# Score rounds one and two of the segment-attention groups two slots earlier in the hand-written order

## The chip, the cores and the metric

The kernel runs on one core of one Trainium2 chip. The metric is the device time of one execution in microseconds. A profile of one execution on the same chip shows every instruction of the engines: TensorE (PE, with its weight loads as PEld), VectorE (DVE), ScalarE (ACT), GpSimd (POOL) and SyncE (SP), which issues the transfers.

## The reference

Four layers run one after the other on x of 2048 tokens by 640 (A, B, A, B), each with a layer norm before it and a residual around it. The change touches only A, attention in four segments of 512 tokens with 32 heads of 20 columns:

```python
for s in range(N):                                  # N = 4 segments of L = 512
    logits = jnp.einsum('bhqd,bhkd->bhqk', qs, ks) * scale + mask
    p = _softmax(logits, axis=-1)
    a_dot = jnp.einsum('bhqk,bhkd->bhqd', p, vs)
    pq = phi(qs)
    num = jnp.einsum('bhld,bhde->bhle', pq, M)
    den = jnp.einsum('bhld,bhd->bhl', pq, z)[..., None] + 1e-06
    outs.append(g * (num / den) + (1.0 - g) * a_dot)
    pk = phi(ks)
    M = M + jnp.einsum('bhld,bhle->bhde', pk, vs)
    z = z + jnp.einsum('bhld->bhd', pk)
return o @ wo
```

The mask is causal within a segment, phi is t + 1 above zero and exp(t) below, g is a gate per head. B (a recurrent attention in 64 steps) is left as it is.

## The kernel before

Layer A takes each segment in 8 groups of four heads, 32 groups in all (`NGR`), and each group in two units, pairs of heads: unit p belongs to group p // 2. The time of a group is cut into four slots. The loop runs over 34 values of g, two halves and two phases, so its slot number is 4g + 2·half + ph; the last two values of g have no group of their own and only finish what is open.

In every slot the loop does its score rounds and then the `filler`, the other work listed for that slot.

Score rounds. For each unit the scores are computed twice. The first time (kind S, rounds 0 to 2, `s_mm` and `s_max`) queries lie on the partitions, and VectorE takes the row maxima. The maxima go through GpSimd (`negmax_rows`) into two spare columns, and `q_with_max` turns Q back with them, giving the tile q2, of which the maximum is a part (the second turn of Q: one matmul with the identity, then four that add the maxima, then a copy). The second time (kind T, rounds 0 to 2, `t_round` and `t_exp`) keys lie on the partitions, TensorE multiplies K's turn with q2, ScalarE takes the exponential into the unit's probability tile PT, and the part on the diagonal is masked. `VISITS` lists which rounds come in which phase: S2, S0, T0 in phase 0, S1, T1, T2 in phase 1. All six use the same three score buffers in PSUM (`psx`). PT comes from the pool `up`, which has three buffers.

Value products. `pv(g)` multiplies both PT tiles of a group with V: 40 matmuls, head by head, so the first 20 read the tile of the first unit only. `norm(g)` then divides and gates on VectorE and GpSimd.

Filler. `SLOTS` says what each slot holds besides: the projections of the next group (QP, KV0, KV1) and the turn of its K (KT), the second turn of Q (Q2), the state's update (UP) and its use (NUM), the value products (PV) of two groups ago, and for the groups 12 to 15, 20 to 23 and 28 to 31 the write-out of a finished 128-token tile of the segment before (otps, YP0, YP1). All of these share two small PSUM buffers (`pg`). `seg_step` puts the loading, norm and turn of the next segment into the first half of a segment's groups.

Order. TensorE runs in the order in which the program is written. ScalarE, VectorE and GpSimd each run in an order by key: the slot number in which the work is written, plus an offset by kind (`A_LAGS`). For ScalarE that gives within slot 3: exponential one, the copy of K's turn, exponential two, the copy of the value products; in slot 0 exponential zero and the copy of Q; in slot 1 exponential one, the copy of q2, exponential two. Waits for data and for buffers are put in by the framework; a tile that finds no free buffer waits for the last reader of the one whose place it takes.

Of the kernel before, what the change touches and what calls it, by code (L numbers as in the profile page):

```python
# [265 lines left out]
def layer_A(nc, tc, C, W, x_src, x_dst, src_is_bf16, nseg=4, out_bf16=False, xb_dst=None, load_w=None, side_loads=None):  # L266
# [4 lines left out]
    NGR = 8 * nseg  # L271
    KOFF = (0, 640, 1024, 512)
    assert not out_bf16
    with ExitStack() as ctx:
# [177 lines left out]
        def k_turn(g):  # L452
            KT_ = pg.tile([128, 4, 128], BF16, name="a_KT", tag="pg")
            for tt in range(4):
                nc.tensor.transpose(KT_[:, tt, :], Kn[g % 2][:, tt, :, :].rearrange("p j s -> p (j s)"), C.identb[:])
            kT = qp4.tile([128, 512], BF16, name="a_kT")
            K("kT").scalar.copy(kT[:], KT_[:].rearrange("p t k -> p (t k)"))
            GS[g]["kT"] = kT
# [15 lines left out]
        def no_tile(step):  # L474
            if step not in NOs:
                NOs[step] = wk.tile([128, 2, 4, 4, 21], F32, name="a_no", tag="a_no")
            return NOs[step]
# [62 lines left out]
        def q_with_max(g):  # L540
            s_ = GS[g]
            N_ = NM[g % 2]
            Q2 = pg.tile([128, 512], F32, name="a_Q2", tag="pg")
            nc.tensor.matmul(Q2[:], lhsT=C.identb[:], rhs=s_["qT"][:], start=True, stop=False, skip_group_check=True)
            for qc in range(4):
                nc.tensor.matmul(Q2[:, 128 * qc:128 * qc + 128], lhsT=N_[:, qc, :, :].rearrange("p j s -> p (j s)"), rhs=C.identb[:],
                                 start=False, stop=(qc == 3), skip_group_check=True)
            q2 = wk.tile([128, 512], BF16, name="a_q2")
            Z = K("q2")
            (Z.vector.tensor_copy if g == NGR - 1 else Z.scalar.copy)(q2[:], Q2[:])  # L550
            s_["q2"] = q2
# [4 lines left out]
        def t_round(p, r, Y):  # L556
            g, pr = divmod(p, 2)
            s_ = GS[g]
            if r == 0:
                s_[("PT", pr)] = up.tile([128, 2, 1280], BF16, name="a_PT", tag="PT")  # L560
            q2, kT, PT = s_["q2"], s_["kT"], s_[("PT", pr)]
            parts = (((0, 0, 512),), ((3, 0, 128), (1, 128, 384)), ((2, 0, 256),))[r]
            width, diag = ((512, 1), (512, 2), (256, 1))[r]
            for n_, (kc, o, w_) in enumerate(parts):
                for e in range(2):
                    j = 2 * pr + e
                    rows = slice(32 * j, 32 * j + 32)
                    nc.tensor.matmul(Y[:, e, o:o + w_], lhsT=kT[rows, 128 * kc:128 * kc + 128], rhs=q2[rows, 128 * kc:512],
                                     start=True, stop=True, tile_position=(32 * j, 0), skip_group_check=True)

        def t_exp(p, r, Y):
            g, pr = divmod(p, 2)
            PT = GS[g][("PT", pr)]
            width, diag = ((512, 1), (512, 2), (256, 1))[r]
            b = 512 * r
            K(f"exp{r}").scalar.activation(out=PT[:, :, b:b + width], in_=Y[:, :, 0:width], func=ACT.Exp, scale=SC)
            dv = PT[:, :, b:b + 128 * diag].rearrange("p e (a q) -> p e a q", q=128)
            if p == 2 * NGR - 1 and r:
                K("dsel").vector.tensor_tensor(out=dv, in0=dv, in1=C.keep[:].unsqueeze(1).unsqueeze(1).to_broadcast([128, 2, diag, 128]), op=ALU.min)
                return  # L580
            K("sel").gpsimd.affine_select(out=dv, in_=dv, pattern=[[0, 2], [0, diag], [1, 128]], compare_op=ALU.is_ge,
                                    fill=0.0, base=0, channel_multiplier=-1)

        def pv(g):
            s_ = GS[g]
            va = s_["va"]
            PV = pg.tile([128, 4, 4, 32], F32, name="a_PV", tag="pg")
            for j in range(4):
                PT = s_[("PT", j // 2)]
                for qc in range(4):  # L590
                    for kc in range(qc + 1):
                        o = KOFF[kc] + 128 * (qc - (kc if kc != 1 else 1))
                        nc.tensor.matmul(PV[:, qc, j, :], lhsT=PT[:, j % 2, o:o + 128], rhs=va[:, kc, j, :],
                                         start=(kc == 0), stop=(kc == qc), skip_group_check=True)
            if g >= NGR - 2:
                s_["osb"] = PV
                return
            K("osb").scalar.copy(no_tile(g + 2)[:, 1], PV[:, :, :, 0:21])
# [78 lines left out]
        K.base = None  # L677

        TPS = (((0, 0), (1, 0), (1, 2)), ((0, 3), (2, 1), (2, 2)), ((1, 3), (3, 0), (3, 3)), ((2, 3), (4, 1), (4, 2)))
        SLOTS = (('otps', 'QP', 'UP'), ('Q2', 'KV0', 'NUM'), ('KV1', 'YP0'), ('KT', 'PV', 'YP1'))  # L680
        VISITS = (('S2', 'S0', 'T0'), ('S1', 'T1', 'T2'))
        OUT_LAG = 4

# [8 lines left out]
        def item(what, g):  # L692
            no, Go = divmod(g - OUT_LAG, 8)
            out = no >= 1 and Go < 4
            if what == "UP" and 0 <= g - 1 < NGR:
                state_up(g - 1)
            elif what == "QP" and g + 1 < NGR:
                proj_q(g + 1)
            elif what == "Q2" and 0 <= g - 1 < NGR - 1:
                q_with_max(g - 1)  # L700
            elif what in ("KV0", "KV1") and g + 1 < NGR:
                proj_kv(g + 1, int(what[2]))
            elif what == "NUM" and g < NGR:
                phi_k(g)
                state_num(g)
            elif what == "KT" and g + 1 < NGR:
                k_turn(g + 1)
            elif what == "PV" and 0 <= g - 2 < NGR:
                pv(g - 2)
                norm(g - 2)  # L710
            elif what == "otps" and out:
                out_stage_a(no - 1, Go)
            elif what in ("YP0", "YP1") and out:
                out_stage_b(no - 1, Go, (int(what[2]),))

        def filler(g, slot):
            K.base = 4 * g + slot + 0.3
            for what in SLOTS[slot]:
                item(what, g)
            if g == NGR and slot == 0:  # L720
                q_with_max(g - 1)
            seg_step(g // 8, g % 8, slot)

        def last_turns(c0, c1):
# [26 lines left out]
        for g in range(NGR + 2):  # L751
            n, G = divmod(g, 8)
            for half in range(2):
                p, tp = 2 * g + half, 2 * g + half - 3
                for ph in range(2):
                    K.base = 4 * g + 2 * half + ph
                    todo = []
                    for what in VISITS[ph]:
                        kind, r = what[0], int(what[1])
                        if kind == "X":  # L760
                            X = s_mask(p, r) if g < NGR else t_tile()
                            if g < NGR:
                                todo.append(("S", p, r, X, 0))
                            if 0 <= tp - 1 < 2 * NGR:
                                todo.append(("T", tp - 1, r, X, 256))
                        elif kind == "S" and g < NGR:
                            todo.append((kind, p, r, s_mask(p, r), 0))
                        elif kind == "T" and 0 <= tp < 2 * NGR:
                            todo.append((kind, tp, r, t_tile(), 0))
                    for step in range(2):  # L770
                        for kind, p_, r, X, o0 in todo:
                            if step == 0 and g >= NGR and (kind, p_) != ("T", 2 * NGR - 3):
                                unread(2)
                            f = (s_mm, s_max)[step] if kind == "S" else (t_round, t_exp)[step]
                            f(p_, r, X, *((o0,) if o0 else ()))
                    if g < NGR and half == 1 and ph == 1:
                        negmax_rows(g)
                    if g == NGR + 1 and half == 1 and ph == 0:
                        last_turns(0, 4)
                        for tt in range(4):  # L780
                            last_oT(tt, 0, 4, K("last").vector if tt < 2 else nc.scalar)
                    filler(g, 2 * half + ph)
                    if side_loads is not None and g < NGR:
                        side_loads[0](4 * g + 2 * half + ph, GS[g]["kT"])
# [651 lines left out]
```

## Time and profile before

| | us |
|---|---|
| median of 3 runs | 2411.46 |
| lowest, highest | 2410.05, 2413.7 |
| the profiled execution | 2409.91 |
| its span in the trace | 2408.0 |

Busy over the whole span: TensorE 2289.4 us (95%), VectorE 1881.2 (78%), ScalarE 1417.7 (59%), GpSimd 750.4 (31%). The two A layers and the two B layers differ: in the page's rows of 40 equal slices ScalarE is at nine tenths in the A layers and at four tenths in B. In timeline rows the columns are start and length in us, engine, line, operation, written tile and what it is read from, shapes, and in brackets idle time of the engine before it and what ended that. `a_T` is a T score tile, `a_S` an S score tile, `a_PT` a probability tile (written by the exponential), `a_Q` and `a_q` the second turn of Q and its copy, `a_KT` and `a_kT` the turn of K and its copy, `a_PV` the value products, `a_no` the copy of those (or of the state's product `a_NUM`), `a_QP` the projection of Q, `a_YP` and `a_otps` the write-out. An exponential 128x1024 wide belongs to round zero or one, 128x512 to round two.

### The profile page before, as it was taken

Reading aid. Unit: us, or ns where it says so; the run is one execution under the profiler, and the core shown is the slowest. Engines: PE = TensorE matmul, PEld = TensorE weight load, DVE = VectorE, ACT = ScalarE, POOL = GpSimd, SP = SyncE. Lnnn points to the kernel's source line nnn. Section 1 sums busy time; section 2 is a strip of 40 time slices with the busy share of each in tenths; the row PEclk is TensorE's granted clock in tenths of the full one; section 3 lists DMA queues with packets and bytes.
Section 4 is the critical chain, followed back from the end, with each engine's and each line's share of the span. In section 5 each row is a group of like instructions: output and inputs, shape, how many; then the busy total and the mean of one; then the engine's idle time right before and its main releaser. Section 6 shows DMA issues by size and latency. Waiting matters only on the chain.

```text
span 2408.0 us, 139298 instructions
## 1 busy us (share of the span) xinstructions
PE 2289.4 (95%) x62308; PEld 1504.2 (62%) x62308; DVE 1881.2 (78%) x4697; ACT 1417.7 (59%) x3198; POOL 750.4 (31%) x1590
## 2 busy tenths in 40 slices
PE   8999999999999999999989999999999999999998
PEld 5566556666666666666656666566666666666666
DVE  8999876777777777777779998677777777777776
ACT  6999974445444444444469999644444444445443
POOL 6677641111111111111146776311111111111111
PEclk9999999999999999999999999999999999999999
DMA  4121271111111111111130210811111111111111
GB/s 168 44 87 62 71 264 26 28 32 30 31 30 30 31 30 32 30 31 26 49 109 19 67 45 33 276 24 26 30 28 27 27 27 28 27 28 27 28 23 21
DMA packets 171219, 123.38 MB, mean 51 GB/s; under 512 B 104684, under 2 KB 155772, under 8 KB 169084
## 3 DMA queue, kind: packets, MB, share of 16 engines
q1 hardware_dynamic: 170194, 114.44, 16.9%
q8 instruction: 487, 7.98, 1.4%
q14 instruction: 112, 0.92, 0.1%
q10 hardware_dynamic: 426, 0.05, 0.0%
HBM read 79.60 MB, written 34.80 MB: 48 GB/s over the span
## 4 chain that ended last, share of the span: by engine, by line
PE 67%; DVE 15%; ACT 10%; DMA 3%; issue 3%; POOL 1%; SPq 1%; ACTq 0%; POOLq 0%; DVEq 0%
PE b_OPS L114 11%; PE b_Ka L114 6%; PE b_Kb L114 6%; PE b_Qa L114 6%; DVE a_nm L143 5%; PE b_tail L114 4%; ACT a_PT L143 4%; PE b_Va L114 4%; PE b_Vb L114 4%; PE b_vtail L114 4%; PE a_S L114 3%; PE b_OPSd L114 2%; PE b_SP L114 2%; PE b_OTP L114 2%; PE b_Qb L114 2%
## 5 line engine op out<-in xcount | busy, mean ns | idle before, releaser
L114 POOL TENSOR_TENSOR b_Pn<-b_E,b_rs 128x200 bf16<-128x200 bf16 x256 | 133.7, 522 | 1080.8 <-DVE b_rs L114 1065.2
L143 DVE TENSOR_REDUCE a_nm<-a_S 128x2 f32<-128x512 f32 (+3 forms) x512 | 395.1, 816 | 45.8 <-PE a_S L114 29.3
L143 ACT ACTIVATE a_PT<-a_T 128x1024 bf16<-128x1024 f32 (+1 forms) x384 | 344.7, 903 | 23.4 <-PE a_T L114 14.8
L114 PEld LDWEIGHTS <-b_HX 128*32 128x32 bf16 x9200 | 241.2, 96 | 136.2 <-DVE b_HX L114 2.7
L114 PEld LDWEIGHTS <-b_R 128*32 128x32 bf16 x8960 | 234.0, 96 | 136.0 <-DVE b_R L114 1.9
L114 PE MATMUL b_OPS<-b_wo,b_OTsb 128*32 128x320 bf16 x8192 | 306.8, 300 | 3.5 <-issue 2.3
L114 PEld LDWEIGHTS <-b_OTsb 128*32 128x32 bf16 x8192 | 208.2, 97 | 72.8 <-DVE b_OTsb L114 19.6
L114 DVE STREAM_TRANSPOSE b_KT<-b_kq 128x512 bf16<-128x512 bf16 x256 | 181.4, 708 | 79.5 <-ACT b_kq L114 78.9
L143 POOL TENSOR_SCALAR_AFFINE_SELECT a_PT<-a_PT 128x256 bf16<-128x256 bf16 x380 | 190.1, 505 | 152.6 <-ACT a_PT L143 151.1
L114 ACT ACTIVATE b_E<-b_SP 128x200 bf16<-128x200 f32 x256 | 86.4, 338 | 234.4 <-DVE b_SP L114 227.6
L114 PEld LDWEIGHTS <-c_J 128*32 128x32 bf16 (+1 forms) x5760 | 182.1, 96 | 66.3 <-issue 8.3
L114 DVE STREAM_TRANSPOSE b_QT<-b_kq 128x256 bf16<-128x256 bf16 (+1 forms) x384 | 183.9, 504 | 38.9 <-ACT b_kq L114 35.5
L114 ACT CAST b_msb<-b_OPS 128x64 bf16<-128x64 f32 x378 | 69.3, 256 | 216.6 <-PE b_OPS L114 216.6
L114 DVE CAST b_OTsb<-b_OTP 128x160 bf16<-128x160 f32 (+1 forms) x384 | 133.6, 376 | 43.0 <-PE b_OTP L114 38.9
L114 ACT CAST b_kq<-b_Ka 128x512 bf16<-128x512 f32 x128 | 75.0, 586 | 125.5 <-PE b_Ka L114 125.5
L114 PE MATMUL b_vtail<-b_wv,c_J 128*32 128x256 bf16 x2560 | 142.2, 274 | 0.7 <-issue 0.4
L114 ACT CAST b_OTsb<-b_OTP 128x320 bf16<-128x320 f32 x256 | 96.5, 429 | 78.1 <-PE b_OTP L114 77.6
L114 PEld LDWEIGHTS <-b_Vth 32*128 32x128 bf16 x4096 | 74.9, 91 | 95.6 <-ACT b_tu L114 38.9
L114 PE MATMUL a_T<-a_q,a_kT 32*128 32x512 bf16 (+3 forms) x1024 | 120.5, 300 | 11.5 <-DVE a_nm L143 6.1
L114 PEld LDWEIGHTS <-c_identb 128*32 128x32 bf16 (+1 forms) x1930 | 99.5, 98 | 47.4 <-issue 17.3
L114 PE MATMUL a_S<-a_kT,a_qT 32*128 32x256 bf16 (+3 forms) x1024 | 114.7, 302 | 1.8 <-ACT a_kT L143 1.6
L114 PE MATMUL b_OPSd<-b_wo,b_OTdef 128*32 128x320 bf16 x2048 | 114.3, 299 | 1.5 <-issue 1.4
(208 smaller groups left out, 5416.4 us busy)
## 6 DMA issues: line engine op xcount, KB each, us to landing
b_wv<-in_B_Wv_dram SPq DMA_DIRECT2D x10, 1024.0 KB
b_wo<-in_B_Wo_dram SPq DMA_DIRECT2D x16, 640.0 KB
b_VT<-b_VTd SPq DMA_DIRECT2D x504, 16.0 KB
b_XO<-xres SPq DMA_DIRECT2D x256, 30.0 KB
b_VTd<-c_J SPq DMA_DIRECT2D x480, 16.0 KB
b_xt<-xres_bf SPq DMA_DIRECT2D x40, 160.0 KB
b_wk<-in_B_Wk_dram SPq DMA_DIRECT2D x20, 256.0 KB
b_wq<-in_B_Wq_dram SPq DMA_DIRECT2D x20, 256.0 KB
```

Of the source, the lines that this page charges most:

```text
L114: r = f(*a, **k)
L143: r = f(*a, **k)
```

## The change

Rounds one and two of kind T of a unit are done one half earlier (`tp = p - 3 + ph`: phase 1 now takes the unit that follows the one of phase 0). So a unit's rounds come in the order one, two, zero, and its PT tile is taken in round one. The second turn of Q moves from slot 1 to the head of slot 0, for all groups alike. The value products of the last two groups move from slot 3 to slot 1, and the last turns with them; the value products of all other groups stay in slot 3. The last unit's round-zero mask moves from GpSimd to VectorE, as those of its other rounds.

```diff
-            if r == 0:
+            if r == 1:
                 s_[("PT", pr)] = up.tile([128, 2, 1280], BF16, name="a_PT", tag="PT")
...
-            if p == 2 * NGR - 1 and r:
+            if p == 2 * NGR - 1:
                 K("dsel").vector.tensor_tensor(out=dv, in0=dv, in1=C.keep[:]...
...
-        SLOTS = (('otps', 'QP', 'UP'), ('Q2', 'KV0', 'NUM'), ('KV1', 'YP0'), ('KT', 'PV', 'YP1'))
+        SLOTS = (('Q2', 'otps', 'QP', 'UP'), ('KV0', 'NUM'), ('KV1', 'YP0'), ('KT', 'PV', 'YP1'))
...
-            elif what == "Q2" and 0 <= g - 1 < NGR - 1:
+            elif what == "Q2" and 0 <= g - 1 < NGR:
                 q_with_max(g - 1)
...
-            elif what == "PV" and 0 <= g - 2 < NGR:
+            elif what == "PV" and 0 <= g - 2 < NGR - 2:
                 pv(g - 2)
                 norm(g - 2)
...
-            if g == NGR and slot == 0:
-                q_with_max(g - 1)
+            if (g, slot) in ((NGR, 1), (NGR + 1, 1)):
+                pv(g - 2)
+                norm(g - 2)
...
-                p, tp = 2 * g + half, 2 * g + half - 3
+                p = 2 * g + half
                 for ph in range(2):
+                    tp = p - 3 + ph
...
-                    if g == NGR + 1 and half == 1 and ph == 0:
+                    if g == NGR + 1 and half == 0 and ph == 1:
                         last_turns(0, 4)
```

## The prediction

> **What bounds the kernel now.** I read the page's busy times first. They say little, because the two layers that change (A, at 0 to 340 us and 1200 to 1535 us of the span) and the two that don't are averaged together. So the first view that counts is the one of busy time by window, cut so that each window is one group of an A layer, as nearly as tenths of a microsecond allow. Columns: window, length, busy time of TensorE matmuls, weight loads, VectorE, ScalarE, GpSimd, then granted clock, DMA share, GB/s.
>
> ```profile
> 68.00:76.50 8.50, 8.47 (x130) 5.26 (x127) 7.42 (x13) 8.01 (x16) 5.48 (x14) 1.00 0.11 33
> 258.60:267.50 8.90, 8.32 (x128) 5.10 (x125) 7.43 (x13) 8.47 (x17) 6.73 (x15) 1.00 0.21 62
> 228.60:238.80 10.20, 9.63 (x149) 6.60 (x146) 9.20 (x17) 9.27 (x20) 7.98 (x17) 1.00 0.38 118
> 186.00:196.00 10.00, 9.30 (x133) 5.95 (x131) 9.90 (x20) 9.25 (x19) 7.80 (x16) 1.00 0.15 45
> ```
>
> In order: a group of the first segment, a bare group of the last segment, a group that also writes out a finished tile, a group that normalizes the next segment. Three engines are full to about nine tenths and more, and there is no slack into which a new wait would fall: what holds one of them up by a microsecond holds the group up by most of it.
>
> Which dependency sets the pace is told by the chain of waits. Here is its piece in a bare group, from the two early score rounds of slot 3 to the projection of Q in the next group's slot 0:
>
> ```profile
> 275.12 0.50 PE a_T L114 x6
> 275.62 0.33 PE a_KT L114 x4
> 275.95 0.99 PE a_PV L114 x40
> 276.94 0.66 PE a_S L114 x8
> 277.61 0.39 PE a_T L114 x2
> ```
>
> TensorE works in its written order: scores, turn of K (a_KT), value products (a_PV), next scores. ScalarE's own row of the same stretch, from the exponential of round zero in slot 2 (274.00) to the same in the next group (282.92):
>
> ```profile
> 274.00 1.07 ACT L143 ACTIVATE a_PT<-a_T 128x1024 bf16<-128x1024 f32 x1
> 274.91 0.35 ACT L143 CAST a_Kn<-a_KV 128x160 bf16<-128x160 f32 x1
> 275.08 0.37 ACT L143 CAST a_vaug<-a_KV 128x160 bf16<-128x160 f32 x1
> 275.55 1.02 ACT L143 ACTIVATE a_PT<-a_T 128x1024 bf16<-128x1024 f32 x1
> 276.47 0.58 ACT L143 COPY a_kT<-a_KT 128x512 bf16<-128x512 bf16 x1
> 276.94 0.61 ACT L143 ACTIVATE a_PT<-a_T 128x512 bf16<-128x512 f32 x1
> 277.43 0.46 ACT L143 COPY a_no<-a_PV 128x336 f32<-128x336 f32 x1
> 278.09 1.02 ACT L143 ACTIVATE a_PT<-a_T 128x1024 bf16<-128x1024 f32 x1 [0.21 <-POOL b_wk L814]
> 279.21 0.59 ACT L143 CAST a_qT<-a_QP 128x512 bf16<-128x512 f32 x1
> 279.82 1.02 ACT L143 ACTIVATE a_PT<-a_T 128x1024 bf16<-128x1024 f32 x1
> 280.74 0.58 ACT L143 CAST a_q<-a_Q 128x512 bf16<-128x512 f32 x1
> ...
> 282.92 1.07 ACT L143 ACTIVATE a_PT<-a_T 128x1024 bf16<-128x1024 f32 x1
> ```
>
> The period is 8.92 us, and ScalarE waits for more than 0.1 us only once in it. The exponentials overlap what follows them (275.55 + 1.02 is 0.10 past 276.47), so a chain of them is counted by starts.
>
> **The change, part by part.** Rounds one and two of a unit (a pair of heads; group g has units 2g and 2g+1) move from slot 2u+7 to slot 2u+5, counted in slots of a quarter group; round zero stays at 2u+6. So a unit's probability tile PT is born at slot 2u+5 instead of 2u+6. It dies with the value products of its group, and those stay in slot 3 two groups later, slot 4g+11. The pool of these tiles has three buffers. Before, the fourth tile, of unit 2g+3, is born at 4g+12, behind those products. Now it is born at 4g+11: in the same slot, and written in the order *ahead of* the products. Four tiles live, three buffers. The exponential of round one of every odd unit must then wait until the tile of unit 2g is free, which is when the first 20 of the 40 value products (heads 0 and 1) are done. This is a new wait on ScalarE, in groups 2 to 31 of each layer. Behind it in ScalarE's order are queued the copy of K's turn, the exponential of round two, the copy of the value products and everything of the next slot; TensorE waits for those, since round zero's score tile needs the buffer that round two's exponential empties (277.61 in the chain, 0.06 after 276.94 + 0.61).
>
> The second turn of Q goes from slot 1 to the head of slot 0, past the out-turn, the projection of Q and the state update on TensorE. Its copy goes on ScalarE from behind exponential one to ahead of exponential zero. That copy is now late by construction: it waits for scores zero and the five turn products.
>
> ```profile
> 275.79 1.16 PE L114 MATMUL a_PV<-a_vaug,a_PT 128*128 128x32 bf16 x40
> ...
> 279.77 0.39 PE L114 MATMUL a_Q<-a_qT,c_identb 128*128 128x512 bf16 x1
> 280.00 0.39 PE L114 MATMUL a_Q<-c_identb,a_NM 128*128 128x128 bf16 x4
> ```
>
> Now one bare group, with zero at the start of slot 2's exponential (274.00). Value products start at 1.79; their first half ends at 1.79 + 0.58 = 2.37; with the 0.04 that the chain shows between engines (275.08 to 275.12), exponential one starts at 2.41 instead of 1.55: **0.86 lost**. Round two's exponential ends 2.00 after that start (277.55 less 275.55), at 4.41; the score tile follows at 4.45 and takes 0.39; the turn takes 0.62 (279.77 to 280.39) and ends at 5.46; its copy starts at 5.50. ScalarE was free at 2.41 + 2.34 = 4.75 (277.89 less 275.55): **0.75 idle**, where 0.21 stood before. From there by starts: copy 0.47 (as 276.47 to 276.94, the same length), exponential zero 0.92, copy of Q 0.61, exponential one 0.92, and from exponential two to the next zero 1.71 as now (280.74 + 0.47 to 282.92). That ends at 10.13, against 8.92: **+1.2 us**.
>
> The Trainium skill (TensorE: Matmul & The Clock Gate, "Wait — 56ns, not 53.3ns?") puts the least start-to-start time of small matmuls at about 25 ns; the trace has 1.16/40 = 29. By the page the 20 products would take 0.50, and the sum below would be some 5 us less, as an estimate.
>
> A group that writes out has more on TensorE between the copy of K's turn and the turn of Q:
>
> ```profile
> 239.36 0.84 PE L114 MATMUL a_YP<-a_wo,a_oT 128*128 128x320 bf16 x5 [0.21 <-ACT a_kT L143]
> ...
> 240.37 0.39 PE L114 MATMUL a_T<-a_q,a_kT 32*128 32x512 bf16 x2
> ```
>
> ```profile
> 241.28 0.69 ACT L143 COPY a_oT<-a_otps 128x640 bf16<-128x640 bf16 x1 [0.77 <-PE a_otps L114]
> 241.87 1.03 ACT L143 ACTIVATE a_PT<-a_T 128x1024 bf16<-128x1024 f32 x1
> ```
>
> The output product waits for that copy, which the new wait delays. K's copy ends 1.50 after exponential one's start (277.05 less 275.55), the score tile comes 1.01 after the product's start, so at 2.55 after exponential one instead of 2.04: +0.5. The out-turn's copy takes 0.6 of ScalarE's row behind the turn's copy, and the projection of Q waits for the buffer of the turn, about 0.3. The cycle is 10.13 + 1.4 = 11.5 against 10.2: **+1.3**. In groups that normalize, the extra ScalarE work (9.25 less 8.47 in the windows) is the exponential of K and the copy of the next segment's turn, which stand just ahead of the two new waits and fall into them; the cycle stays near 10.13, but such groups (VectorE at 9.90 of 10.00) take 9.4 to 10.0 already: **+0.5**, between 0.1 and 0.9. Groups of the first segment have less on ScalarE (8.01), and TensorE sets part of their cycle: together with the bare ones, **+1.0**.
>
> Of groups 2 to 31, ten write out (13–15, 21–23, 28–31), ten normalize or stand at a change of segment (9–12, 16–20, 24), ten are bare (2–8, 25–27): 10 × (1.3 + 0.5 + 1.0) = 28 us a layer, 56 us for both.
>
> What costs nothing: the turn of Q needs the row maxima a slot sooner. They are there: GpSimd's last step on them ends at 277.41, and the turn now comes at 274.00 + 4.84 = 278.84 at the soonest.
>
> ```profile
> 277.14 0.27 POOL L143 TENSOR_TENSOR a_NM<-a_nm,a_NM 128x16 bf16<-128x16 f32 x1
> ```
>
> With that cover gone the turn would wait up to the few tenths by which the maxima are late. No DMA moves within the groups. At the end of the layer the residual loads of the last segment are issued a slot sooner, with all that is around them, and keep their place in SyncE's queue:
>
> ```profile
> 331.51 1.04 SPq L738 DMA_DIRECT2D a_oTx<-in_A_x_dram  x2
> ```
>
> The last unit's mask moves from GpSimd to VectorE, at about the same length.
>
> At the end of a layer two slots go, and the last products come sooner.
>
> ```profile
> 325.89 7.10 ACT L143 ACTIVATE a_PT<-a_T 128x1024 bf16<-128x1024 f32 x9 [0.44 <-POOL a_NM L143]
> ...
> 332.99 1.16 PE L114 MATMUL a_PV<-a_vaug,a_PT 128*128 128x32 bf16 x40
> ```
>
> Nine exponentials set that end. Two of them (0.9 + 0.5) now lie before it, done earlier on engines that idle while the layer starts. But the next one then waits for the last turn of Q, which those two used to cover. Gain 0.5 to 1.4 a layer; I take 0.5, so 1 in all. The waits also show what goes: the row below is TensorE's total over 100 to 300 us, and it vanishes, but into the longer ScalarE cycle.
>
> ```profile
> PE a_NUM L114 <- ACT a_q L143: 4.8, 15, 0.4
> ```
>
> Sum: the profiled execution took 2409.9 us (span 2408.0); plus 56, less 1, is 2465. The median of the runs shown is 2411.46, 1.5 above that execution, so **2466 us**.
>
> **The rivals.** *The wait is longer:* the buffer may count as free only after all 40 value products. Half of them more is 0.58 a group, 60 groups: +35, 2501. For it speaks only that the trace has no such wait to show its grain; against, that heads 0 and 1 alone read the tile. Chance 0.11.
>
> *One wait hides the other:* if TensorE, idle meanwhile, comes back early enough for the turn's copy, only the 0.86 remains, and in the full VectorE groups half of it: 2 × (20 × 0.86 + 10 × 0.4) = 42, or less where score buffers come free sooner: 2440 to 2452. Chance 0.17.
>
> *The clock drops in the new pauses.* The same group (number 9) in both layers:
>
> ```profile
> 94.70:106.00 11.30, 10.30 (x136) 6.03 (x133) 9.95 (x18) 9.31 (x19) 7.99 (x17) 0.85 0.14 40
> 1295.10:1304.90 9.80, 9.01 (x139) 5.87 (x136) 9.77 (x18) 9.29 (x19) 7.97 (x16) 1.00 0.11 35
> ```
>
> With a mean clock of 0.85 it took 1.5 us longer. If every second changed group caught such a drop, 30 × 1.5 = 45 more: 2511. The Trainium skill (TensorE: Matmul & The Clock Gate, "Part 1: The HAM clock gate") lets the clock fall only after an idle window of about 3.4 us, and no pause above comes near; by it, this adds nothing. The trace doesn't bear that out cleanly, as the dipping window has only 1.0 us of matmul idleness in all. Chance 0.05.
>
> *Faster:* the new wait never bites, because ScalarE reaches exponential one later than the first 20 products end. It decides at 0.86 us of lag. Then the vanished wait of the state product (4.8 us in 200, some 10 over both layers) and the ends (1 to 2.8) are the gain: 2398. Against it: ScalarE was there 0.10 after its previous work (275.45 to 275.55), with no lag at all. Chance 0.05. That the two halves cancel, or that the order is not what the lines say, so that the time is the same: 0.02.
>
> **How the numbers follow.** Forecast as reckoned 0.60, the rivals 0.17, 0.11, 0.05, 0.05, 0.02. About 0.2%, 5 us, can be told from no change here. Slower: 0.93; faster 0.05; same 0.02. The forecast's own range is 2452 to 2485 (group costs of 0.75 to 1.3). Taking in the hidden wait below (2440) and the longer one above (2501) leaves out the clock drops and the faster cases: 2440 to 2502.
>
> **What would show it.** Right: in the waits, ScalarE's exponentials wait for the value products some 60 times, 0.8 us each, about 50 us; its copy of the turn waits for the turn some 50 times; the state product no longer waits; bare groups have a period near 10.1 us, those that write out near 11.5; busy times of all engines stay, layers B too. Wrong: no wait of an exponential on the value products, or group periods under 9.2 us in the bare groups. A wait of 1.4 us there would mean that all 40 products are waited for; a clock under 1.00 across the A layers, the third rival.

## The result, and the profile after

| | before | after |
|---|---|---|
| median of 5 runs, us | 2411.46 | 2493.99 |
| lowest, highest | 2409.46, 2414.31 | 2491.11, 2502.25 |
| the profiled execution | 2409.91 | 2493.99 |
| its span | 2408.0 | 2492.3 |

The change makes the kernel slower: ratio 1.0343, 95% interval 1.033 to 1.0357, or +82.5 us. The forecast was 2466 (+55) in a range of 2440 to 2502; the forecast's own range, without the rivals, was 2452 to 2485, and the measured time lies above it.

First the windows of single groups, with the columns of those before (length, busy time of TensorE, weight loads, VectorE, ScalarE, GpSimd, granted clock, DMA share, GB/s): a group of the first segment, a bare one of the last, one that writes out, and two that normalize in which the clock fell.

```profile
68.70:78.70 10.00, 8.84 (x124) 5.64 (x124) 7.57 (x13) 8.09 (x16) 5.70 (x14) 1.00 0.09 28
299.70:309.80 10.10, 9.02 (x122) 5.72 (x122) 7.84 (x12) 8.23 (x17) 5.99 (x12) 1.00 0.09 28
239.90:251.70 11.80, 10.11 (x143) 6.97 (x144) 8.32 (x16) 9.03 (x18) 7.24 (x15) 1.00 0.24 79
107.20:118.80 11.60, 10.68 (x133) 6.75 (x135) 10.03 (x20) 9.42 (x19) 6.98 (x18) 0.85 0.13 39
196.50:208.00 11.50, 10.31 (x122) 6.45 (x120) 9.74 (x18) 9.14 (x18) 7.45 (x15) 0.85 0.13 40
```

ScalarE has the same work in a bare group as before (8.23 against 8.47, by the cut of the window) in a group that is 1.25 us longer. Its own row in that bare group shows what it waits for:

```profile
298.52 1.02 ACT L143 ACTIVATE a_PT<-a_T 128x1024 bf16<-128x1024 f32 x1 [1.18 <-PE a_PV L114]
299.44 0.58 ACT L143 COPY a_kT<-a_KT 128x512 bf16<-128x512 bf16 x1
299.90 0.62 ACT L143 ACTIVATE a_PT<-a_T 128x512 bf16<-128x512 f32 x1
300.39 0.46 ACT L143 COPY a_no<-a_PV 128x336 f32<-128x336 f32 x1
301.54 0.58 ACT L143 CAST a_q<-a_Q 128x512 bf16<-128x512 f32 x1 [0.69 <-PE a_Q L114]
302.03 1.03 ACT L143 ACTIVATE a_PT<-a_T 128x1024 bf16<-128x1024 f32 x1
...
306.06 1.06 ACT L143 ACTIVATE a_PT<-a_T 128x1024 bf16<-128x1024 f32 x1
...
308.68 1.02 ACT L143 ACTIVATE a_PT<-a_T 128x1024 bf16<-128x1024 f32 x1 [1.18 <-PE a_PV L114]
```

Exponential one waits for the value products, the copy of Q's turn for the turn, and nothing else waits. The period is 308.68 less 298.52, 10.16. The chain of waits says of how many products:

```profile
307.17 0.59 PE a_T L114 x6
307.76 0.33 PE a_KT L114 x4
308.09 0.51 PE a_PV L114 x20
...
308.68 1.02 ACT a_PT L143
```

Scores, K's turn, twenty products, and then the exponential: the buffer is free at the half. Summed over the run, the waits on ScalarE and the two on TensorE that grew most:

```profile
ACT a_PT L143 <- PE a_PV L114: 64.3, 59, 1.4
ACT a_q L143 <- PE a_Q L114: 43.8, 55, 2.6
PE a_YP L114 <- ACT a_kT L143: 24.3, 22, 1.1
PE a_S L114 <- ACT a_PT L143: 10.9, 23, 0.6
```

Before, TensorE's wait of the output product for the copy of K's turn was 4.4 us in 21 times, and no exponential waited for products.

**Where the time went.** I cut each A layer at the starts of the 32 copies of K's turn; the period of a group is the time from one to the next. From first to last copy the layers went from 297.7 and 302.0 us to 336.8 and 341.9: +79. From the last copy to the first matmul of B's tail it is 26.3 before and 26.9 after in both layers: +1. The B layers went from 870.1 and 868.0 to 874.3 and 868.2: +4. Together 84, as the two profiled executions differ (2493.99 less 2409.91). To keep the falls of the clock apart (short stretches of some 3.5 us or more at a granted clock of about 0.50: ten in the A layers, against two before), I take of each group the shorter of its two layers. These undisturbed groups are 71 us longer over both layers; the other 8 of the 79 are what disturbed groups have more, the falls above all.

| groups of a layer | forecast, each | measured, each (undisturbed) |
|---|---|---|
| first segment (2–8) | +1.0 | +1.24 |
| bare, last segment (25–27) | +1.0 | +1.25 |
| normalizing, change of segment | +0.5 | +0.85 |
| writing out | +1.3 | +1.52 |

### The profile page after: what moved, and what is told of

It is laid out like the page before. It is cut to its first block, busy times and chain, and to the rows that moved or that the text cites. A ratio compares the mean times of both kernels' runs of the same rounds, so it can differ in the third digit from the quotient of the medians.

```text
span 2492.3 us, 139221 instructions
## 1 busy us (share of the span) xinstructions
PE 2321.7 (93%) x62246; PEld 1530.8 (61%) x62308; DVE 1896.1 (76%) x4699; ACT 1417.8 (57%) x3198; POOL 751.6 (30%) x1588
## 4 chain that ended last, share of the span: by engine, by line
PE 71%; DVE 11%; ACT 10%; DMA 3%; issue 3%; POOL 1%; SPq 1%; ACTq 0%; POOLq 0%; DVEq 0%
PE b_OPS L114 11%; PE b_Ka L114 6%; PE b_Kb L114 5%; PE b_Qa L114 5%; PE b_tail L114 4%; PE b_Va L114 4%; PE b_Vb L114 4%; ACT a_PT L143 4%; PE a_S L114 4%; PE b_vtail L114 4%; DVE a_nm L143 3%; PE a_QP L114 3%; PE b_OTP L114 2%; PE b_SP L114 2%; PE b_OPSd L114 2%
## 5 line engine op out<-in xcount | busy, mean ns | idle before, releaser
L143 ACT ACTIVATE a_PT<-a_T 128x1024 bf16<-128x1024 f32 (+1 forms) x384 | 334.3, 891 | 83.4 <-PE a_PV L114 64.3
L143 POOL TENSOR_SCALAR_AFFINE_SELECT a_PT<-a_PT 128x512 bf16<-128x512 bf16 x378 | 191.5, 516 | 226.9 <-ACT a_PT L143 221.2
L114 PE MATMUL a_S<-c_negu,c_identb 128*128 128x128 bf16 (+1 forms) x768 | 104.2, 240 | 25.7 <-DVE a_nm L143 11.5
L114 PE MATMUL a_T<-a_q,a_kT 32*128 32x128 bf16 (+3 forms) x1024 | 119.5, 300 | 7.5 <-ACT a_PT L143 2.1
```

Source lines behind the costliest of these rows:

```text
L114: r = f(*a, **k)
L143: r = f(*a, **k)
```

## The experiments

Theory at the outset: the fourth live tile is the cause, through ScalarE's wait, and the turn in slot 0 adds its own wait. Rivals: the waits only show a schedule that is longer for another reason, or the clock does it. In all diffs, lines that are left out are "...".

**1. Value products out of the way.** The changed kernel with the value products one slot sooner, ahead of the fourth tile.

```diff
-        SLOTS = (..., ('KV1', 'YP0'), ('KT', 'PV', 'YP1'))
+        SLOTS = (..., ('KV1', 'PV', 'YP0'), ('KT', 'YP1'))
```

> The changed kernel with one edit: the value products of two groups ago stand in slot 2 instead of slot 3, ahead of round one of the odd unit, so that the third probability tile is free before a fourth is asked for. Theory (three buffers for four live tiles is the main loss): the waits of the exponentials on the value products (59 waits, 64.3 us) go to nearly none, the wait of the turn's copy (57, 45.2 us) stays, a bare group falls from 10.16 to about 9.3 us, a writing one from 11.73 to about 10.7, the whole to about 2430 us (2420 to 2445). Rival (the loss is in the new pairing of rounds of different units in one slot, which holds the score buffers longer, and the waits only show it): some other wait takes the place of the one removed, time stays above 2470 us.

Measured: 2486.06 us, ratio 1.0307 (1.0279 to 1.0335). The wait of the exponential on the products is gone from the list, yet only 8 us came back; my number missed by 40 to 65, and the rival's (some other wait in its place, above 2470) came out. Exponentials now wait for scores, 41.7 us in 53 times, against 11.4 in 31 in the changed kernel. The bare group went from 10.16 to 9.59 and no further. TensorE's and ScalarE's rows there:

```profile
304.23 0.40 PE L114 MATMUL a_KT<-c_identb,a_Kn 128*128 128x128 bf16 x4
305.36 0.40 PE L114 MATMUL a_S<-c_negu,c_identb 128*128 128x128 bf16 x4 [0.73 <-DVE a_nm L143]
```

```profile
307.31 0.58 ACT L143 CAST a_q<-a_Q 128x512 bf16<-128x512 f32 x1 [1.02 <-PE a_Q L114]
```

In slot 3 the 40 products had filled the time until VectorE's row maxima freed a score buffer. With them gone TensorE stands there idle for 0.73, all that follows is late, and the copy of the turn waits 1.02 instead of 0.69. Writing groups became longer still (11.88 against 11.73): there the output product now follows the value products at once, on the same two small PSUM buffers, and waits for their copy (11.6 us in 22 times). So moving the products takes away one wait and uncovers another. It doesn't undo the cause, and it leaves open whether the pairing of rounds costs by itself; experiment 5 decides that.

**2. The turn's copy behind round zero's exponential.** A one-number change of ScalarE's order.

```diff
-          ... "q2": 0.1, ...
+          ... "q2": 0.25, ...
```

> The changed kernel with one edit: the copy of the second turn of Q gets the offset 0.25 instead of 0.1, so that on ScalarE it stands behind the exponential of round zero and not ahead of it. Nothing moves on TensorE. Theory (the turn's copy at the head of slot 0 is a second loss of its own): the 45 us that ScalarE waits for the turn fall to under 15 us, the time falls by about 27 us to 2467 us (2455 to 2475), with the waits on the value products as they are. Rival (ScalarE's pause is filled by whatever comes next in any order, since the buffer wait sets the group): no change, 2494 us within 6.

Measured: 2523.32 us, ratio 1.0464 (1.0433 to 1.0495), 29 us slower than the change, outside both numbers. The wait of the copy is gone (1.2 us left), and the bare group of the last segment is 10.16 as before the edit. First one more row of ScalarE in the changed kernel, then the rows of this one, of ScalarE and of TensorE:

```profile
303.45 1.51 ACT L143 ACTIVATE a_PT<-a_T 128x1024 bf16<-128x1024 f32 x2
```

```profile
311.82 1.02 ACT L143 ACTIVATE a_PT<-a_T 128x1024 bf16<-128x1024 f32 x1 [1.17 <-PE a_PV L114]
...
314.30 1.02 ACT L143 ACTIVATE a_PT<-a_T 128x1024 bf16<-128x1024 f32 x1
315.22 0.58 ACT L143 CAST a_q<-a_Q 128x512 bf16<-128x512 f32 x1
315.92 0.58 ACT L143 CAST a_qT<-a_QP 128x512 bf16<-128x512 f32 x1
316.75 1.51 ACT L143 ACTIVATE a_PT<-a_T 128x1024 bf16<-128x1024 f32 x2 [0.24 <-PE a_T L114]
```

```profile
313.87 0.39 PE L114 MATMUL a_T<-a_q,a_kT 32*128 32x512 bf16 x2
314.19 0.39 PE L114 MATMUL a_Q<-a_qT,c_identb 128*128 128x512 bf16 x1
314.42 0.39 PE L114 MATMUL a_Q<-c_identb,a_NM 128*128 128x128 bf16 x4
314.64 1.24 PE L114 MATMUL a_QP<-a_xnT,a_wq_pad 128*128 128x512 bf16 x4
315.72 0.38 PE L114 MATMUL a_S<-c_negu,c_identb 128*128 128x256 bf16 x2
316.04 0.39 PE L114 MATMUL a_S<-a_kT,a_qT 32*128 32x384 bf16 x4
316.26 0.49 PE L114 MATMUL a_T<-a_q,a_kT 32*128 32x128 bf16 x6
```

From one exponential one (311.82) to the next (316.75) it is 4.93; in the changed kernel, 298.52 to 303.45, also 4.93. In that stretch TensorE's row (round zero, turn, projection of Q, scores) has no gap, so it is as long as ScalarE's row with its 0.69 of waiting. In these groups the wait for the turn was therefore worth nothing by itself: two paths of equal length. Elsewhere the edit costs: groups of the first segment and normalizing ones that no fall touched are about 0.2 longer, and writing ones 0.7 in most cases (12.44 against 11.73), where the copy of the out-turn, which comes behind in the order, waits instead, 32.7 us in 24 times, and the projection of Q for it. Undisturbed groups give some 22 of the 32 us by which the A layers grew (an estimate: six of the 31 groups were hit in both layers, and take the cost of their class); the rest are falls of the clock, 17 of them against 10.

**3. Both edits.** 

> Both edits together on the changed kernel: value products in slot 2, turn's copy behind the exponential of round zero. Theory (two losses that add, nothing else): both waits are gone and the time is that of the kernel before or a little under it, 2400 to 2418 us; bare groups at 8.9 us, writing ones at 10.2. Rival (the pairing of rounds costs by itself): above 2430 us.

Measured: 2510.75 us, ratio 1.041 (1.0384 to 1.0436). The theory that the two waits were the whole cost (2400 to 2418) has fallen, and the rival's number (above 2430) came out again. Bare groups stay at 9.59, writing ones at 12.59, and exponentials wait for scores 71.6 us in 96 times, against 14.8 in 57 before. That left the question which part of the change to take back, not which wait.

**4. The turn alone.** The kernel before, with the second turn of Q at the head of slot 0 and nothing else.

```diff
-        SLOTS = (('otps', 'QP', 'UP'), ('Q2', 'KV0', 'NUM'), ...)
+        SLOTS = (('Q2', 'otps', 'QP', 'UP'), ('KV0', 'NUM'), ...)
...
-            elif what == "Q2" and 0 <= g - 1 < NGR - 1:
+            elif what == "Q2" and 0 <= g - 1 < NGR:
...
-            if g == NGR and slot == 0:
-                q_with_max(g - 1)
```

> The kernel before with one part of the change alone: the second turn of Q at the head of slot 0, for all groups, its copy ahead of the exponential of round zero; the score rounds stay where they were. Theory: the tile pool is not touched, so no waits on the value products; the turn's copy is waited for about as in the changed kernel, some 0.3 to 0.75 us a group, and the state product no longer waits: 2425 to 2440 us. Rival (the copy's place costs nothing where the buffer wait is absent, since scores zero come sooner): 2405 to 2415 us.

Measured: 2425.60 us, ratio 1.0067 (1.0044 to 1.0089), at the lower end of what was expected. The copy waits in the bare group just as long as in the changed kernel, but the period is only 9.08 (8.91 before); writing groups have 10.60 (10.18).

```profile
286.49 0.59 ACT L143 CAST a_q<-a_Q 128x512 bf16<-128x512 f32 x1 [0.69 <-PE a_Q L114]
```

**5. Four tiles.** The changed kernel with a buffer for each of the four live units. Rounds one and two get a tile of their own (`a_PU`, four buffers), round zero keeps PT (three), and three other pools give up one buffer each for the space.

```diff
+        up2 = pool("a_unit2", 4)
...
-                s_[("PT", pr)] = up.tile([128, 2, 1280], BF16, name="a_PT", tag="PT")
+                s_[("PU", pr)] = up2.tile([128, 2, 768], BF16, name="a_PU", tag="PU")
+            if r == 0:
+                s_[("PT", pr)] = up.tile([128, 2, 512], BF16, name="a_PT", tag="PT")
```

> The changed kernel with the wait's cause taken away and the value products left in slot 3: the probabilities of rounds one and two get tiles of their own, four of them, those of round zero keep three; room is made by one buffer less for Q, for K's turn and for phi of Q, which the order leaves free in time. Theory, as the first runs leave it (the fourth tile is the loss; the turn in slot 0 alone costs about 14 us; moving the products to slot 2 failed because it uncovered the wait of the next scores on VectorE's maxima): no waits on the value products, bare groups near 9.1 us, writing ones near 10.6, the whole 2418 to 2440 us. Rival (the pairing of rounds of two units in a slot costs by itself, whatever the tiles): 2460 to 2490 us, with waits of the scores on the maxima or of the exponentials on the scores in place of those on the value products.

Measured: 2432.38 us, ratio 1.0101 (1.0079 to 1.0123), as the theory expected. The products stay in slot 3, and no exponential waits for them:

```profile
284.41 1.02 ACT L143 ACTIVATE a_PU<-a_T 128x1024 bf16<-128x1024 f32 x1
285.33 0.58 ACT L143 COPY a_kT<-a_KT 128x512 bf16<-128x512 bf16 x1
...
287.43 0.58 ACT L143 CAST a_q<-a_Q 128x512 bf16<-128x512 f32 x1 [0.69 <-PE a_Q L114]
```

The bare group has 9.08, the number of experiment 4 to the hundredth, and so does the wait of the copy. So the fourth tile's buffer is worth about 60 us (2493.99 less 2432.38 is 62; each set against the kernel before in its own series, 82.5 less 24.0 is 59). Of that some 50 are in groups that no fall touched, and most of the rest are falls of the clock, 4 in place of 10. With room for the tile the shift of rounds one and two costs nothing in the bare groups, so the rival of experiments 1 and 3, that the pairing costs by itself, has fallen there; writing groups keep 0.2 (10.80 against the 10.60 of experiment 4). What is left (24 us above before) is mostly the turn, 14 to 17 by experiment 4.

**6 and 9. Which half of the products.** Two orders of the heads: the second unit's first, and alternating, so that the first tile comes free after 30 products.

```diff
-            for j in range(4):
+            for j in (2, 3, 0, 1):      # experiment 6
+            for j in (0, 2, 1, 3):      # experiment 9
```

> The changed kernel with the value products of a group in the order heads 2, 3, 0, 1 instead of 0, 1, 2, 3, so that the tile that is waited for is read last. It leaves everything else. Theory (the exponential waits for the last reader of that tile alone, and ScalarE's loop passes it on in full): the waits on the value products grow by 0.58 us each, 59 of them, 34 us, to about 2528 us. Rival (the buffer counts as free only after all forty products anyhow, or the loop has slack there): 2494 us within 8.

> The changed kernel with the value products' heads made in the order 0, 2, 1, 3, so that the first of the two probability tiles is free after 30 of the 40 products, not after 20. Theory (the exponential waits for the first tile that comes free, whichever it is): ten products of 0.029 us more a group, so the mean wait of an exponential on the value products goes from 1.09 to about 1.35 us (total in the trace from 64 to about 80 us), bare groups from 10.16 to about 10.4 us, and the time to about 2511 us (2503 to 2518). Rival (the wait ends with something other than the count of products, such as the turn of K or the end of all 40): total wait stays within 3 us of 64, time 2494, within the scatter of the half-clock stretches (some 8 us).

Measured for 6: 2505.90 us, ratio 1.0404 (1.0379 to 1.0429), between the two numbers. The wait grew from 64.3 to 66.3 us only, and the chain again has twenty products ahead of the exponential:

```profile
306.23 0.51 PE a_PV L114 x20
```

So the new tile takes whichever buffer comes free first, not that of one certain unit. That was a wrong step of mine: swapping the halves does not lengthen the wait. Groups that no fall touched keep their periods within 0.11 of those of the changed kernel; the 12 us more come with 15 falls of the clock against 10, and partly from outside the groups.

Measured for 9: 2523.50 us, ratio 1.0477 (1.0449 to 1.0505). The wait is 83.4 us in 60 times, 1.39 each, where 1.35 was expected; bare groups have 10.41, where 10.4 was expected, and the chain has thirty products:

```profile
321.75 0.75 PE a_PV L114 x30
```

```profile
312.18 1.02 ACT L143 ACTIVATE a_PT<-a_T 128x1024 bf16<-128x1024 f32 x1 [1.43 <-PE a_PV L114]
```

The mechanism is shown: ten products more, 0.25 us more period. The total came out 12 us over my number. The excess stands in the normalizing groups, which are 20.6 and 21.8 us a layer above before, against 9.0 and 10.0 in the changed kernel; but it is the clock, not a longer answer to the wait. There are 18 falls in the A layers against 10, twelve of them in normalizing groups against three, and the normalizing groups that no fall touched are 0.17 to 0.25 longer, like most of the others (0.25). That, in 58 groups, is 14 or 15 of the 29 us by which the A layers grew. The mean granted clock shows it; it was 0.992 in the changed kernel:

```profile
core 0: 2516.2 us, clock 0.983
```

**7. The pause filled.** The changed kernel with the products of heads 2 and 3 made twice in groups 2 to 29, so that TensorE works while ScalarE waits. The sums are the same; only the work is more.

```diff
-            for j in range(4):
+            for j in (0, 1, 2, 3) + ((2, 3) if 2 <= g < NGR - 2 else ()):
```

> The changed kernel with the value products of heads 2 and 3 made twice over in groups 2 to 29 (the second time overwrites the first with the same numbers): 0.58 us more of full-size work on TensorE just where it pauses for the exponential of round one. Theory (the drops of the clock in the A layers, ten against two before, come from these pauses and cost 1.5 us each, some 12 us; the pause of 0.55 us or more hides the added work): drops go to four or fewer, time 2480 to 2490 us. Rival (the drops don't depend on it, or the added work is in the way): as many drops, 2494 to 2525 us.

Measured: 2482.11 us, ratio 1.0302 (1.0275 to 1.0328): with more work it is 12 us faster than the change. The wait is the same, and so are the periods (bare 10.16, writing 11.73, normalizing 10.48):

```profile
306.15 1.66 PE L114 MATMUL a_PV<-a_vaug,a_PT 128*128 128x32 bf16 x60
```

```profile
306.90 1.02 ACT L143 ACTIVATE a_PT<-a_T 128x1024 bf16<-128x1024 f32 x1 [1.18 <-PE a_PV L114]
```

What changed is the clock. These are the rows of mean granted clock, first of the changed kernel, then of this one:

```profile
core 0: 2492.3 us, clock 0.992
```

```profile
core 0: 2480.0 us, clock 0.996
```

At half clock, 0.8% of the span off is 40 us at the lower clock, and 0.4% is 20. By the trace of the A layers, ten stretches became five (one more than the theory's upper bound), and the groups' excess over the shorter layer fell from 16.6 to 6.0 us. So the third rival of the prediction was real, at a small size.

**8. The end alone.** The kernel before with the last two groups' products, and the last turns, two slots sooner; score rounds and the turn of Q stay.

```diff
-            elif what == "PV" and 0 <= g - 2 < NGR:
+            elif what == "PV" and 0 <= g - 2 < NGR - 2:
...
+            if (g, slot) in ((NGR, 1), (NGR + 1, 1)):
+                pv(g - 2)
+                norm(g - 2)
...
-A_LAGS = {"dsel": 0.5, ...
+A_LAGS = {"dsel": 0.25, ...
```

The offset puts the last unit's masks on VectorE ahead of the last division.

> The kernel before with the end of the change alone: the value products of the last two groups in slot 1 instead of slot 3 and the last turns with them; score rounds and turn stay; the masks of the last unit on VectorE go ahead of the last division (offset 0.25), as that order needs it. Read in the trace: from the last copy of K's turn to the first product of layer B, 26.3 us before, 26.9 in the changed kernel. Theory (that end is set by nine exponentials in a row, not by where the products stand): 26.0 to 26.5 us, total within 2410 plus or minus 5. Rival (the products' place is what shortens the end): 25.5 us or less.

Measured in one execution: 2418.52 us. The end of a layer, from the last copy of K's turn to B's tail, took 29.7 and 30.7 us, against 26.3. Both numbers missed: this run is 3 to 4 us a layer longer there. The last six exponentials wait, which in the kernel before stand in a row of nine with 0.44 ahead of it:

```profile
329.54 5.04 ACT L143 ACTIVATE a_PT<-a_T 128x1024 bf16<-128x1024 f32 x6 [1.97 <-POOL a_AD L143]
```

But in both ends the granted clock also fell to about half, for 7.2 and 10.4 us, where neither the kernel before nor the changed one has a fall:

```profile
329.90:337.10 7.20, 7.20 (x81) 4.13 (x78) 2.27 (x7) 5.68 (x8) 2.65 (x5) 0.53 0.56 200
1531.60:1542.00 10.40, 10.15 (x106) 5.32 (x107) 3.19 (x10) 6.14 (x8) 4.34 (x8) 0.51 0.79 275
```

So how much of the 3.4 and 4.4 us is the order, and how much the clock, this one execution doesn't tell.

**10 and 11. A better place for the turn, with four tiles.** Experiment 10 has Q2 last in slot 0, with its copy behind that of the projection (`"q2": 0.55`); experiment 11 leaves Q2 at the head and puts its copy behind round zero's exponential (`"q2": 0.25`).

> Four tiles, and the second turn of Q last in slot 0 (behind the projection of Q and the state update), its copy on ScalarE behind the copy of the projection. Theory (what is left of the four-tile version's 24 us is the turn that stands at the head of slot 0 and whose copy waits 0.7 us for round zero's scores): the copy no longer stands ahead of round zero's exponential, but now rounds one and two's scores come right behind it: TensorE waits about 0.4 us for it, bare groups 9.1 to 9.5 us instead of 9.08, time 2425 to 2450. Rival (any place but the head is better): bare groups at 8.9, time 2410 to 2420.

> Four tiles, the turn of Q at the head of slot 0 as in the change, its copy on ScalarE one place later, behind round zero's exponential. Theory: round zero's exponential starts some 0.5 us sooner, the copy waits for nothing, and rounds one and two's scores still find their Q in time, since the projection of Q lies between on TensorE: bare groups 8.9 to 9.0 us instead of 9.08, time 2415 to 2428, against 2432 with the copy ahead. Rival (as in the three-tile kernel, where the same edit left bare groups alone and cost the writing groups 0.7 us each, by the copy of the out-turn that then comes late): 2440 to 2455.

Measured for 10: 2494.35 us, ratio 1.0349 (1.0334 to 1.0365). TensorE waits 0.40 for the copy, as the theory had it, and bare groups have 9.59, just above its 9.1 to 9.5:

```profile
308.52 0.50 PE L114 MATMUL a_T<-a_q,a_kT 32*128 32x128 bf16 x6 [0.40 <-ACT a_q L143]
```

But the total missed by 44 us: groups of the first segment have 10.3 on average and normalizing ones 11.7. There VectorE's row maxima wait for scores, 118.9 us in 142 times, against 37.3 in 78 in experiment 5; that this is the cause is not shown.

Measured for 11: 2452.96 us, ratio 1.0183 (1.0166 to 1.0201). Bare groups have 9.03 (expected 8.9 to 9.0), but the rival had the total. Writing groups went from 10.80 to 11.52, and the copy of the out-turn waits:

```profile
ACT a_oT L143 <- PE a_otps L114: 26.7, 24, 1.6
```

No version that was tried beats the kernel before. The nearest that keeps the sooner scores is experiment 5, at 1.0101.

## Why the prediction was right, and where its sizes were off

**The mechanism** came out step by step: 59 waits of an exponential for value products (some 60 forecast), 1.09 us each; 55 of the copy for the turn (some 50); the state product's wait for the copy of Q gone from the list; ScalarE's busy time 1417.8 (1417.7). Experiment 5 shows that the buffer is the cause, 9 that it is counted by products, and the x20 of the chain that half of them are enough: the rival of all forty has fallen. The length of the wait alone would not have told, since 1.18 in a bare group lies between the 0.86 forecast and the 1.4 that was the sign of all forty.

**The range** held by more than the mechanism. Measured is 2493.99, above the 2452 to 2485 that the forecast had for itself (by its own group costs, 45 to 78 us, that range would be some 3 us higher, and still too low). It lies inside 2502 only because the range took in the rival of all forty products, which was wrong. The way, the cause and the place were forecast; that the number fell inside is in part luck.

**The bare group** was reckoned at 10.13 and measured at 10.16, leg by leg: from exponential zero to one 2.62 (2.41 forecast), to the copy of Q 3.02 (3.09), to the next exponential zero 4.52 (4.63). That the sum is so close is luck in part: its legs are off by +0.21, −0.07 and −0.11, which cancel. The first is off because the forecast took the start of the products, 1.79, from a timeline row that overlaps the row ahead of it; by the chain they started at 1.95 before, and they start at 2.03 in the changed kernel (308.09 less 306.06); twenty of them then took 0.51 instead of 0.58, with 0.08 instead of 0.04 behind them. And one term of that sum was misread. The 0.75 of waiting for the turn (0.69 measured) was counted as a cost on ScalarE's row. Experiment 2 took it away and gained nothing there, and experiment 4 prices the moved turn at 0.17 a bare group, since TensorE's row beside it is as long. Had I added up both rows, I would have known that only the buffer can be bought back.

**The waits** were forecast at 0.86 each, 50 us in all, and came to 64.3. In the bare group 1.18 stands for 0.86: 0.10 of the difference is the pause that was there before (ScalarE is free 1.45 after exponential zero in both kernels, and exponential one started at 1.55), and 0.21 is the leg above. The period was right all the same, since the later legs came out shorter by almost as much.

**The sum** for the groups was 56, and is 71 undisturbed. The mis-sized terms, by the table above: first segment and bare 1.24 for 1.0 (+5 over 20 groups; I took a lower number because ScalarE has less work there, but a wait for a buffer doesn't shrink with it), writing groups 1.52 for 1.3 (+4), normalizing 0.85 for 0.5 (+7; it lies inside the bounds of 0.1 to 0.9, at their end). The forecast also spoke of three engines at nine tenths and more; VectorE was at 7.43 of 8.90 us in the bare group, 0.83, so the bare group had some slack there.

**The end of the layer** was put at −0.5 each and is +0.6. That the next exponential would wait for the turn was in the prediction; its size was not. Experiment 8 shows no gain from the products' place without the sooner scores, but with the clock at half there it gives no price, so what became of the 0.5 stays open.

**The clock**, a rival at 0.05, holds in part: about 8 us of the 82.5 are what disturbed groups have more than before, and experiment 7 gains 12 by filling the pause. The rival's size (every second group) did not come.

**Layers B** were to stay. The first is 4.2 us longer, the second 0.2; more than half of the 4 us come in one step, the clock has no fall there in the changed kernel (one before), and the other kernels scatter there between 869.8 and 877.8 with no order that I see. This stays open. TensorE's busy time, which was also to stay, is 2321.7 against 2289.4; part of it are the matmuls at half clock, and the rest I have not traced.

## What to carry to other kernels

When work is moved sooner, count the tiles alive at the moment when the moved step takes its buffer, in written order and with the last reader's place in the same slot; one buffer short costs a wait across engines in every turn of the loop, here about 60 us of 2411. Price a wait only after adding up the other engine's row beside it: waits of 0.69 and 1.18 us stood in the same bare group, and taking the first away gained nothing there. Before a difference of some ten microseconds is put down to the order, count the falls of the clock in both runs: experiments 2, 6 and 9 had 15 to 18 of them against 10. And where a pause goes, look for what had been hidden in it: products that leave their slot uncover a wait for the score buffers of 0.73 us.

## What the runs showed of the hardware that I had not expected

The clock of TensorE falls in a kernel whose pauses are short. These are windows of 3.40 us in the changed kernel, each pair first the window just ahead of a fall, then the fall:

```profile
103.80:107.20 3.40, 2.40 (x57) 1.72 (x56) 3.33 (x8) 2.37 (x5) 2.08 (x5) 0.99 0.00 0
107.20:110.60 3.40, 3.18 (x17) 1.52 (x19) 3.11 (x5) 2.43 (x6) 2.78 (x8) 0.50 0.14 32
195.90:199.30 3.40, 2.58 (x57) 1.76 (x55) 3.33 (x9) 2.42 (x5) 2.63 (x5) 1.00 0.03 5
199.30:202.70 3.40, 3.18 (x16) 1.81 (x16) 2.17 (x4) 2.05 (x4) 2.34 (x7) 0.50 0.28 85
```

The granted clock is 0.50 for about one window and then 1.00 again. Ahead of it matmuls were busy 2.40 of 3.40 us and 2.58 of 3.40, or 0.71 and 0.76, most of them the short value products, and the longest pauses were 0.62 and 0.82. Such a fall costs a group 1.1 to 1.7 us (group 17 of the first layer, the second fall shown, has 12.16 against 10.52 in the second layer). A window so thin is not enough for a fall: this one, with 2.25 of 3.40, has none at its end.

```profile
328.40:331.80 3.40, 2.25 (x57) 1.90 (x54) 2.37 (x5) 2.19 (x6) 2.69 (x6) 1.00 0.00 0
```

The Trainium skill (TensorE: Matmul & The Clock Gate, "Part 1: The HAM clock gate") lets the clock fall after at least one idle window of about 3.4 us, on a grid that runs freely. The length of the window agrees with these rows; that it must be idle does not, since about seven tenths of it were busy. That the grid runs freely would fit with which groups are hit (2, 4, 9 and 17 in the first layer; 1, 8, 18, 21, 25 and 30 in the second), and with thin windows that are spared, but no run here tests it.
